# Another hand-written order for the first eleven stretches, and another way to store the last two rows, in a one-core attention kernel

## The chip, the cores and the metric

The kernel runs on one core of a Trainium2 chip. The metric is the time that the device needs for one execution, in microseconds; the profile and the trace come from one such execution, recorded by the hardware profiler. TensorE (PE) multiplies matrices, VectorE (DVE), ScalarE (ACT) and GpSimd (POOL) work on tiles, and SyncE (SP) issues most of the DMAs. ACT and POOL can issue DMAs as well.

## The reference

```python
xn = layernorm(x)                                   # x: 1 x 2048 x 640
q  = (xn @ wq).reshape(1, 2048, 32, 192)            # 32 heads of 192
k, v = k_cache[:, :, -512:], v_cache[:, :, -512:]   # a window of 512 keys
p  = softmax(q @ k.T * 192 ** -0.5)
s  = (p @ v).reshape(1, 2048, 32 * 192) @ wo
# a second branch on xn: the two tokens with the largest xn @ w_r go through a small
# gated network (640 -> 1536 -> 640) and are added back to xn
g  = silu(branch(xn))
out = x + s * g
```

All inputs are bfloat16, the sums are made in float32.

## The kernel before, in words

The 2048 tokens are 16 tiles of 128. The 32 heads are 8 groups of four, each of two pairs of heads. A step i is a group, a block of 512 tokens (four tiles) and a pair; the first steps are i = 0 and 1 for the first block and the two pairs, 2 and 3 for the second block, and so on. A step has four units, one for each token tile: unit n belongs to step n // 4. Units are taken together in stretches: S.0 has units 0 and 1, S.1 units 2 and 3, and each later stretch three units (S.2 has 4, 5, 6; S.3 has 7, 8, 9). There are 86 stretches.

Nothing is scheduled by a planner. Every engine works its instructions in the order in which the program writes them, and the program writes them by a list of short words. For the stretches 0 to 10 that list is the string `FIRST`, written by hand; from 11 on the function `stretch` writes it, and the end is again by hand (`LAST`). The words are these, with the engine in brackets; a last letter a, v or g chooses ScalarE, VectorE or GpSimd, or, for loads, the queue:

- `x.b.lo.hi`: load token tiles lo to hi of block b (SP, or ACT with an a). `k`, `v`, `wq`, `wo`: loads of the keys, the values and the two weights.
- `bn.n.c` (VectorE, half the statistics of tile n) or `as.n` (ScalarE, the statistics of tile n in two passes), `sq`, `rc`, `pw` (the inverse root), `ap.n` (the normalised tile). `sx` and `ex` load ScalarE's tables. `z` is a product of zeros on TensorE.
- `turn.n` (TensorE transposes of a tile and a copy), `xT.lo.hi` and `kT` (transposes by DMA), `kt.0` and `kt.1` (TensorE transposes of the first keys and a copy).
- `q.i.c` (a third of the projection of step i, five products with 512 columns; with lo and hi, a half with 256 columns), `qe.i.c` its eviction to `qT`.
- `S.j`: the scores of the stretch, two heads for each unit; `M.n.h` the maximum of a row (VectorE); `E.n.h` the exponential (ScalarE); `P.n` the transpose of the result by DMA (SP); `R` the reciprocal of the sums.
- `O.n` (products with the values) and `Oe.n` its eviction; `T.j` the transpose of a stretch's outputs by DMA (SP), `T.j.lo.hi` of a part of it; `W.w` (products with `wo` for a row of token tiles, two halves of 320 columns) and `We.w` the eviction into the running sum.

PSUM has eight buffers in two pools: six (`ps_p`) for scores, for both halves of a `W`, and for each `q`, `O` or `turn` that asks for one (a g on `q` and `O`), and two (`ps_f`) for the others. A buffer is given out in the written order of the words that release it: the next product that asks for one gets the buffer whose last reader stands first in the list, and waits for that reader.

The last row of token tiles is `W.127`, in three parts of 256, 192 and 192 columns; the row ahead of it is `W.126`, in two parts of 320. Their evictions are `w_out` (lines 423 to 453 of the kernel before): a product with the gate and a sum, and the store of the row to HBM.

Of the kernel before, what the change touches and what calls it, by code (L numbers as in the profile page):

```python
# [21 lines left out]
def kernel(ctx, tc, A_x, A_k_cache, A_v_cache, A_wq, A_wo, B_x, B_w_r, B_w_gate, B_w_up, B_w_down, out):  # L22
    nc = tc.nc
    P = 128
    _, S, D = A_x.shape
# [397 lines left out]
    def w_out(w, e="v"):  # L423
        b, u = divmod(w, 4)
        g, t5, _ = steps[b * PAIRS]
        n = t5 * 4 + u
        parts = w_open.pop(w)
        if g < NG - 1:
            for w_ps, lo, hi in parts:
                acc = s_acc[:, n, lo:hi]  # L430
                if g == 0:
                    copies[e](out=acc, in_=w_ps)
# [8 lines left out]
        for k, (w_ps, lo, hi) in enumerate(parts):
            cs = slice(lo, hi)
            by_v = e == "v" or last and k > 0
            prod = w_ps if by_v else t[:, cs]
            nc.vector.tensor_tensor(out=prod, in0=w_ps, in1=xn[:, n, cs], op=ALU.mult)  # L445
            if e != "g":
                (nc.vector if by_v else nc.gpsimd).tensor_tensor(out=o[:, cs], in0=prod, in1=s_acc[:, n, cs], op=ALU.add)  # L447
# [478 lines left out]
```

## The time and the profile before

| | us |
|---|---|
| median of three runs | 790.01 (789.75 to 790.72) |
| the profiled execution, time | 789.15 |
| the profiled execution, span of the trace | 787.4 |
| TensorE busy | 781.8 (99%) |
| VectorE busy | 621.7 (79%) |
| ScalarE busy | 479.4 (61%) |
| granted TensorE clock | 0.999 |

The span runs from the first to the last recorded instruction. The time of the same execution is longer by what lies around it. A busy TensorE isn't always at work: the end of a product is modelled, and a product that waits in the pipeline for a short while can be counted as busy. So in the dense part the starts of the products are read, not their busy time.

### The profile page before, as it was taken

The numbers are of one execution on the slowest core, as the hardware profiler recorded it, in microseconds if no ns is written. First come the engines' busy times: TensorE is split into PE (matmuls) and PEld (weight loads), VectorE is DVE, ScalarE is ACT, GpSimd is POOL, SyncE is SP. The second block draws the span as 40 slices with busy tenths as digits, with TensorE's granted clock in tenths as the row PEclk, the third lists the DMA queues.
The fourth block names the chain that finished last, engine by engine and source line by source line (L and its number), as shares of the span: only waits on it lengthen the run. The fifth ranks groups of instructions, "written<-read, shape, count | busy, mean of one in ns | idle before, by whom it ended". The sixth has DMA issues, their size and how long they took to land.

```text
span 787.4 us, 15694 instructions
## 1 busy us (share of the span) xinstructions
PE 781.8 (99%) x5767; PEld 482.8 (61%) x5767; DVE 621.7 (79%) x1238; ACT 479.4 (61%) x1299; POOL 179.5 (23%) x198
## 2 busy tenths in 40 slices
PE   8999999999999999999999999999999999999998
PEld 4566656666666666566666655666566666556666
DVE  7976678988888777777777777777788988777786
ACT  8975766565556655565665556565667865565652
POOL 3230000000010000000000699960000000165966
PEclk9999999999999999999999999999999999999999
DMA  9999998899889999999998899779997799997996
GB/s 262 214 202 229 204 199 132 164 175 202 166 147 219 184 195 217 142 221 198 191 222 144 181 180 188 158 141 174 202 172 138 143 193 184 183 194 152 177 167 148
DMA packets 453133, 143.80 MB, mean 183 GB/s; under 512 B 421358, under 2 KB 452720, under 8 KB 453056
## 3 DMA queue, kind: packets, MB, share of 16 engines
q1 hardware_dynamic: 447696, 138.04, 94.0%
q10 hardware_dynamic: 4672, 3.08, 1.4%
q0 software_dynamic: 688, 1.68, 0.9%
q8 instruction: 45, 0.74, 0.4%
q14 instruction: 32, 0.26, 0.1%
HBM read 39.98 MB, written 2.62 MB: 54 GB/s over the span
## 4 chain that ended last, share of the span: by engine, by line
PE 95%; DMA 2%; DVE 1%; ACT 1%; issue 0%; SPq 0%; POOL 0%; DVEq 0%
PE q_ps L317 26%; PE w_ps L420 26%; PE o_ps L372 21%; PE sc L331 14%; PE sc L338 8%; DMA oT<-o_sb 1%; DMA x_in<-in_A_x_dram 1%; ACT pexp L353 1%; DVE nm L346 0%; DVE stats L172 0%; POOL fin_o L447 0%; PE gu_ps L590 0%; ACT o_sb L385 0%; PE y_ps L627 0%; DVE fin_t L445 0%
## 5 line engine op out<-in xcount | busy, mean ns | idle before, releaser
L353 ACT ACTIVATE pexp<-sc,nm 128x512 bf16<-128x512 f32 x512 | 348.5, 697 | 264.1 <-issue 231.7
L346 DVE TENSOR_REDUCE nm<-sc 128x1 f32<-128x512 f32 x512 | 314.9, 682 | 70.9 <-PE sc L338 70.7
L317 PE MATMUL q_ps<-xnT,wq_p 128*128 128x512 bf16 (+1 forms) x985 | 225.4, 374 | 0.5 <-DMA wq_p<-in_A_wq_dram 0.5
L420 PE MATMUL w_ps<-wo_g,oT 128*128 128x320 bf16 (+1 forms) x1542 | 223.0, 298 | 0.1
L420 PEld LDWEIGHTS <-oT 128*128 128x128 bf16 x1542 | 150.4, 98 | 69.5 <-DMA oT<-o_sb 0.4
L372 PE MATMUL o_ps<-v_sb,pT 128*128 128x192 bf16 x2048 | 184.8, 246 | 0.0
L372 PEld LDWEIGHTS <-pT 128*128 128x128 bf16 x2048 | 171.4, 98 | 14.0 <-issue 2.8
L317 PEld LDWEIGHTS <-wq_p 128*128 128x128 bf16 x985 | 89.7, 98 | 122.8 <-issue 33.3
L387 DVE TENSOR_TENSOR o_sb<-o_ps,lsum 128x384 bf16<-128x384 f32 x240 | 132.0, 556 | 41.3 <-PE o_ps L372 22.7
L331 PE MATMUL sc<-kT,qT 128*128 128x512 bf16 x512 | 125.5, 379 | 0.1
L434 DVE TENSOR_TENSOR s_acc<-s_acc,w_ps 128x320 f32<-128x320 f32 x192 | 92.5, 483 | 30.7 <-PE w_ps L420 30.7
L353 ACT ACTIVATION_READ_ACCUMULATOR pexp<-sc,nm 128x1 f32 x512 | 110.2, 215 | 0.0
L309 ACT ACTIVATE qT<-q_ps 128x512 bf16<-128x512 f32 (+1 forms) x180 | 98.7, 604 | 0.0
L331 PEld LDWEIGHTS <-qT 128*128 128x128 bf16 x512 | 48.5, 98 | 42.0 <-issue 1.5
L338 PE MATMUL sc<-kT,qT 64*128 64x512 bf16 x512 | 70.2, 380 | 0.0
L338 PEld LDWEIGHTS <-qT 64*128 64x128 bf16 x512 | 18.0, 94 | 46.7 <-issue 35.8
L664 POOL TENSOR_TENSOR s_acc<-s_acc,xn 128x640 f32<-128x640 f32 x16 | 22.9, 1434 | 103.0 <-DVE s_acc L434 102.9
L643 POOL TENSOR_TENSOR xn<-xn,yh 128x640 bf16<-128x640 bf16 x32 | 44.6, 1394 | 2.7
L633 POOL DMA_DIRECT2D y_d<-y_sb x4 | 2.2, 544 | 181.2 <-DVE y_sb L630 181.2
L510 POOL DMA_DIRECT2D c_d<-cand x1 | 0.7, 725 | 162.8 <-DVE cand L508 162.8
L665 POOL TENSOR_TENSOR s_acc<-s_acc,x_fin 128x640 f32<-128x640 f32 x16 | 22.4, 1400 | 61.4 <-DVE s_acc L434 54.3
L642 POOL TENSOR_SCALAR yh<-y_bc,oh 128x640 bf16<-128x640 bf16 x32 | 25.6, 800 | 5.2 <-DMA y_bc<-y_d 3.6
(110 smaller groups left out, 234.1 us busy)
## 6 DMA issues: line engine op xcount, KB each, us to landing
wo_g<-in_A_wo_dram SPq DMA_DIRECT2D x15, 480.0 KB, 4.3
wq_p<-in_A_wq_dram SPq DMA_DIRECT2D x14, 480.0 KB, 4.6
v_sb<-in_A_v_cache_dram SPq DMA_DIRECT2D x15, 384.0 KB, 4.3
k_raw<-in_A_k_cache_dram SPq DMA_DIRECT2D x28, 192.0 KB, 3.2
pT<-pexp SPq DMA_TRANSPOSE x256, 3.6
x_fin<-in_A_x_dram SPq DMA_DIRECT2D x16, 160.0 KB, 2.7
wgu<-in_B_w_gate_dram SPq DMA_DIRECT2D x15, 128.0 KB, 3.3
wgu<-in_B_w_up_dram SPq DMA_DIRECT2D x15, 128.0 KB, 3.6
```

Source lines behind the costliest of these rows:

```text
L309: nc.scalar.activation(out=out, in_=in_, func=ACT.Copy, scale=scale)
L317: nc.tensor.matmul(q_ps, lhsT=wq_of[g * PAIRS + pr][:, dc, c * P:(c + 1) * P], rhs=xnT[:, t5 * 4 + lo:t5 * 4 + hi, dc, :], start=(dc == 0) ...
L331: nc.tensor.matmul(sc_of[n][hh], lhsT=qT_of[i][:, 2 * hh, u * P:(u + 1) * P], rhs=kp[:, :, 2 * hh, :], start=True, stop=False)
L338: nc.tensor.matmul(sc_of[n][hh], lhsT=qT_of[i][hs, 1, u * P:(u + 1) * P], rhs=kp[hs, :, 1, :], start=False, stop=True)
L346: nc.vector.tensor_reduce(out=nm_of[j][:, c:c + 1], in_=sc_of[n][hh], axis=AX.X, op=ALU.max, negate=True)
L353: nc.scalar.activation(out=pe_of[n][:, hh, :], in_=sc_of[n][hh], func=ACT.Exp, bias=nm_of[j][:, c:c + 1], scale=1.0, accum_out=l_of[j][:, ...
L372: nc.tensor.matmul(ps[:, hh, :], lhsT=pT_of[n][:, hh, jj, :], rhs=v_sb[:, hh, jj, :], start=(jj == 0), stop=(jj == NJ - 1))
L387: nc.vector.tensor_tensor(out=osb_of[j][:, m], in0=ps, in1=l_of[j][:, 2 * m:2 * m + 2].unsqueeze(2).to_broadcast([P, 2, Dh]), op=ALU.mult)
L420: nc.tensor.matmul(w_ps, lhsT=oT_of[j][:, stretches[j].index(n), c % 3, :], rhs=wo_of[g][:, c, lo:hi], start=(c == 0), stop=(c == CPG - 1))
L434: nc.vector.tensor_tensor(out=acc, in0=acc, in1=w_ps, op=ALU.add)
L642: nc.gpsimd.tensor_scalar(out=yh, in0=M["y_bc"][:, j, :], scalar1=M["oh"][:, n, j:j + 1], scalar2=0.0, op0=ALU.mult, op1=ALU.add)
L643: nc.gpsimd.tensor_tensor(out=xn[:, n, :], in0=xn[:, n, :], in1=yh, op=ALU.add)
```

## The change

`FIRST` is written in another order. The words are the same work, with few exceptions: the first block's tiles 0 and 1 come by two loads, tile 0 by ACT's queue and tile 1 by SP's; tiles 2 and 3 of the second block come in one load in place of two; `q.1.1` and `q.6.0` are split into halves and `q.1.0` no longer is; some evictions go to the other of ScalarE and VectorE, and some products to the other PSUM pool; of the loads that ACT issues late in this part, `k.3.1` and `wo.1.0` go to SP. In `w_out`, the last row's second and third parts are both multiplied ahead of their sums and are stored by one DMA, where there were two, and the row ahead of it is stored in two halves.

```diff
+        def add(k, prod, cs):
+            by_v = e == "v" or last and k > 0
+            (nc.vector if by_v else nc.gpsimd).tensor_tensor(out=o[:, cs], in0=prod, in1=s_acc[:, n, cs], op=ALU.add)
+            if last and k == 0 or w == NW - 2:
+                nc.sync.dma_start(out=out_v[:, n, cs], in_=o[:, cs])
+
+        sums = []
         for k, (w_ps, lo, hi) in enumerate(parts):
...
             if e != "g":
-                (nc.vector if by_v else nc.gpsimd).tensor_tensor(out=o[:, cs], in0=prod, in1=s_acc[:, n, cs], op=ALU.add)
-            if last:
-                (nc.scalar if k > 0 else nc.sync).dma_start(out=out_v[:, n, cs], in_=o[:, cs])
+                sums.append((k, prod, cs))
+            if not (last and k == 1):
+                for args in sums:
+                    add(*args)
+                sums = []
...
-        if not last:
+        if last:
+            nc.scalar.dma_start(out=out_v[:, n, DA:D], in_=o[:, DA:D])
+        elif w < NW - 2:
```

The part of `FIRST` ahead of S.0, and the stretches 0 to 7, which the prediction walks through:

```diff
-z.1 z.1 z.1 sx z.1 z.1 x.0.0.2 x.0.2.4 as.1 k.0.1 k.0.0 bn.0.0 bn.0.1 bn.3.0 sq.0.1 sq.1.2 as.2 rc.0.1 rc.1.2 wq.0 x.1.1.2 ap.0.v ex ap.1.v bn.3.1 pw.2.4 turn.0.v turn.1.1.v kt.0.a kt.1.v q.0.0.0.2.g qe.0.0.0.2.a ap.3.g bn.5.0 x.1.0.1 x.1.3.4 x.1.2.3 q.0.1.0.2.g k.1.1 bn.5.1 qe.0.1.0.2.a q.0.2.0.2.g k.1.0 qe.0.2.0.2.a turn.3.1.a as.6 ap.2.v bn.7.0 bn.7.1 turn.2.v 
-S.0 bn.4.0 v.0 bn.4.1 wq.1 q.0.0.2.4.g qe.0.0.2.4.a x.2.0.4 kT.1 M.0.0 E.0.0 pw.4.8 q.0.2.2.4.g M.0.1 qe.0.2.2.4.v E.0.1 P.0 q.0.1.2.4 qe.0.1.2.4.a M.1.0 M.1.1 E.1.0 E.1.1 ap.4.v 
-S.1 q.1.2 ap.5.g M.2.0 ap.7.g E.2.0 M.2.1 q.1.0.2.4 ap.6.g xT.4.6 q.1.0.0.2.g bn.10.0 qe.1.2.a M.3.0 M.3.1 R.0 bn.10.1 xT.6.8 E.2.1 qe.1.0.0.2.a qe.1.0.2.4.a q.1.1 P.2 bn.11.0 O.0 bn.11.1 bn.8.0 E.3.0 E.3.1 qe.1.1.a Oe.0.v P.1 bn.8.1 
-S.2 x.3.0.4 v.1 q.2.1.0.2 as.9 M.4.0 M.4.1 q.2.0 M.6.0 E.4.0 pw.8.12 E.4.1 q.2.2.g M.5.0 qe.2.1.0.2.a E.5.0 qe.2.0.v M.6.1 ap.10.g E.6.0 ap.9.g P.3 E.6.1 M.5.1 q.3.1 qe.2.2.v ap.8.v R.1 ap.11.g O.2 qe.3.1.v Oe.2.v E.5.1 
-S.3 M.8.0 M.7.0 P.4 P.5 M.8.1 q.2.1.2.4 M.7.1 R.2 xT.8.10 M.9.0 as.13 bn.15.0 M.9.1 E.8.0 E.7.0 E.8.1 q.3.2 bn.14.0 xT.10.12 E.7.1 P.6 qe.2.1.2.4.a q.3.0.g qe.3.0.a qe.3.2.v E.9.0 E.9.1 O.1.g O.5.g O.4.g Oe.4.a Oe.1.v P.8 as.12 Oe.5.v O.3 
-S.4 P.7 bn.15.1 M.10.0 q.4.1 M.11.0 M.12.0 M.11.1 Oe.3.a q.4.0 P.9 M.10.1 qe.4.1.v E.10.0 M.12.1 E.11.0 T.0 E.11.1 q.5.0.g E.10.1 wo.0.0 wo.0.1 T.2.0.1 E.12.0 E.12.1 R.3 qe.4.0.a O.8.g O.7 P.10 Oe.7.a qe.5.0.v T.1 Oe.8.v R.4 bn.14.1 pw.12.16 
-S.5 ap.12.g O.6 M.13.0 P.11 E.13.0 M.15.1 Oe.6.a M.15.0 E.15.0 E.15.1 q.4.2 M.13.1 P.12 q.5.2.g M.14.1 M.14.0 qe.4.2.v O.9 E.13.1 Oe.9.a qe.5.2.v E.14.0 W.0 We.0.v E.14.1 
-S.6 M.17.0 P.13 M.17.1 ap.14.g M.16.1 O.10 M.18.1 Oe.10.a M.16.0 ap.13.g E.17.0 q.5.1 E.17.1 qe.5.1.v T.2.1.3 E.16.0 R.5 O.12 O.11.g Oe.11.a M.18.0 E.18.0 Oe.12.a E.16.1 W.1 O.13.g We.1.v E.18.1 ap.15.g xT.13.16 xT.12.13 W.2 We.2.v P.15 Oe.13.a 
+z.1 x.0.0.1.a sx bn.0.0 x.0.1.2 as.1 x.0.2.4 bn.0.1 x.1.0.1 sq.0.1 bn.3.0 z.1 k.0.0 rc.0.1 sq.1.2 z.1 rc.1.2 z.1 ap.0.v ap.1.v k.0.1 bn.3.1 bn.4.0 z.1 as.2 turn.1.1.a turn.0.v ex pw.2.4 kt.0.v wq.0 kt.1.a x.1.1.2 x.1.2.4 ap.3.v q.0.0.0.2.g q.0.2.0.2.g q.0.1.0.2.g qe.0.0.0.2.a k.1.0 bn.4.1 bn.7.0 bn.7.1 ap.2.g k.1.1 qe.0.2.0.2.a bn.5.0 qe.0.1.0.2.a turn.2.1.a wq.1 turn.3.1.v 
+S.0 bn.5.1 q.0.2.2.4.g M.0.0 as.6 pw.4.8 E.0.0 M.0.1 q.0.0.2.4.g E.0.1 qe.0.2.2.4.v v.0 q.0.1.2.4 qe.0.1.2.4.a ap.4.g qe.0.0.2.4.v M.1.0 E.1.0 ap.6.g x.2.0.4 q.1.1.0.2 M.1.1 E.1.1 
+S.1 qe.1.1.0.2.a ap.5.v M.2.0 M.3.0 E.2.0 kT.1 M.2.1 bn.8.0 q.1.0.g ap.7.g qe.1.0.a q.1.1.2.4.g P.0 bn.10.0 M.3.1 E.3.0 E.2.1 R.0 bn.11.0 q.1.2 xT.4.6 xT.6.8 P.2 qe.1.1.2.4.v qe.1.2.a E.3.1 bn.10.1 O.0 Oe.0.a bn.11.1 
+S.2 M.4.0 M.4.1 bn.8.1 q.2.1.0.2 q.2.0 as.9 P.1 E.4.0 M.5.0 x.3.0.4 M.5.1 v.1 pw.8.12 q.2.2.g E.4.1 qe.2.0.v ap.10.g E.5.0 P.4 E.5.1 P.3 M.6.0 qe.2.2.a E.6.0 qe.2.1.0.2.v q.3.1.g M.6.1 O.2 q.2.1.2.4.g P.5 E.6.1 qe.2.1.2.4.a ap.8.g qe.3.1.v ap.11.g R.1 Oe.2.v ap.9.v 
+S.3 M.7.0 q.3.2 M.7.1 M.9.0 xT.8.10 as.13 E.7.0 M.8.0 M.9.1 O.4 q.3.0.g E.7.1 xT.10.12 qe.3.2.a R.2 O.3.g E.8.0 M.8.1 O.1.g E.9.0 O.5 Oe.4.v qe.3.0.a E.9.1 P.6 E.8.1 Oe.3.v P.7 P.8 Oe.1.v bn.15.0 Oe.5.v 
+S.4 bn.15.1 T.0 q.4.1 M.10.0 as.14 M.12.1 M.12.0 E.10.0 R.3 q.4.0 M.11.0 E.12.0 P.9 qe.4.0.v E.12.1 qe.4.1.a q.5.0.g O.7 E.11.0 wo.0.0 M.10.1 wo.0.1 bn.12.0 E.10.1 T.2.0.1 M.11.1 qe.5.0.v E.11.1 O.8 
+S.5 bn.12.1 Oe.7.a pw.12.16 P.10 Oe.8.a M.13.0 M.15.0 T.1 P.12 M.13.1 O.6 q.4.2 E.13.0 Oe.6.v P.11 q.5.2.g M.14.0 M.15.1 E.13.1 O.9 E.14.0 M.14.1 R.4 E.14.1 W.0 qe.5.2.a qe.4.2.v ap.15.g O.10 E.15.0 We.0.v ap.12.g Oe.9.v E.15.1 Oe.10.v 
+S.6 T.2.1.3 M.16.0 O.12 ap.14.g M.17.0 q.5.1 ap.13.a E.16.0 Oe.12.v M.16.1 P.13 P.15 xT.12.13 M.17.1 M.18.1 M.18.0 E.16.1 E.17.0 O.11 E.17.1 W.1 E.18.0 E.18.1 R.5 W.2 We.1.a xT.13.16 Oe.11.v We.2.v P.14 qe.5.1.v T.3 
+S.7 M.19.0 M.20.0 O.13 Oe.13.a E.19.0 T.4 q.6.1 k.2.1.a M.21.0 q.6.2 qe.6.1.v P.16 qe.6.2.a O.14.g M.21.1 M.19.1 E.21.0 M.20.1 q.7.0 E.19.1 Oe.14.v E.20.0 E.21.1 qe.7.0.a O.15 P.17 E.20.1 q.6.0.0.2.g W.4 W.3 P.18 Oe.15.v q.6.0.2.4 qe.6.0.0.2.a P.19 We.4.a We.3.a 
...
```

More of the change, by code (lines that the diff above doesn't have):

```diff
@@ L440, in w_out @@
         o = fin_pool["o"].tile([P, D], BF16, name="fin_o")
+        def add(k, prod, cs):
[4 more added lines that the diff above has]
+        sums = []
         for k, (w_ps, lo, hi) in enumerate(parts):
             cs = slice(lo, hi)
-            by_v = e == "v" or last and k > 0
-            prod = w_ps if by_v else t[:, cs]
+            prod = w_ps if e == "v" or last and k > 0 else t[:, cs]
             nc.vector.tensor_tensor(out=prod, in0=w_ps, in1=xn[:, n, cs], op=ALU.mult)
             if e != "g":
-                (nc.vector if by_v else nc.gpsimd).tensor_tensor(out=o[:, cs], in0=prod, in1=s_acc[:, n, cs], op=ALU.add)
-            if last:
-                (nc.scalar if k > 0 else nc.sync).dma_start(out=out_v[:, n, cs], in_=o[:, cs])
+                sums.append((k, prod, cs))
[3 more added lines that the diff above has]
+                sums = []
         if e == "g":
             nc.gpsimd.tensor_tensor(out=o, in0=t, in1=s_acc[:, n, :], op=ALU.add)
-        if not last:
+        if last:
+            nc.scalar.dma_start(out=out_v[:, n, DA:D], in_=o[:, DA:D])
+        elif w < NW - 2:
             (nc.gpsimd if w < NW - 8 else nc.scalar if w < NW - 6 else nc.sync).dma_start(out=out_v[:, n, :], in_=o)
@@ L876 @@
-S.7 q.6.1 M.19.1 M.19.0 E.19.0 M.20.0 q.6.0 qe.6.0.v P.14 T.4 M.21.0 M.20.1 M.21.1 E.19.1 T.3 q.6.2.g k.2.1.a qe.6.1.a O.14 O.15.g R.6 E.20.0 q.7.1.g E.20.1 Oe.14.a P.17 qe.6.2.a E.21.0 Oe.15.v q.7.0 P.16 E.21.1 P.19 W.3 P.18 W.4 qe.7.1.v R.7 qe.7.0.v We.3.v O.19 We.4.a wq.2.a
-S.8 wq.3.a O.16 Oe.19.v M.22.0 v.2.a M.23.1 E.22.0 Oe.16.v k.3.0.a M.23.0 P.20 E.23.0 wo.1.0.a E.23.1 k.3.1.a T.5 M.22.1 M.24.0 P.21 q.7.2 E.24.0 O.17 Oe.17.v E.22.1 P.22 k.2.0.a W.5 qe.7.2.v M.24.1 We.5.a O.20 P.23 W.6 O.21 We.6.a E.24.1 Oe.20.a Oe.21.a O.18.g Oe.18.v P.24
@@ new lines @@
+S.6 T.2.1.3 M.16.0 O.12 ap.14.g M.17.0 q.5.1 ap.13.a E.16.0 Oe.12.v M.16.1 P.13 P.15 xT.12.13 M.17.1 M.18.1 M.18.0 E.16.1 E.17.0 O.11 E.17.1 W.1 E.18.0 E.18.1 R.5 W.2 We.1.a xT.13.16 Oe.11.v We.2.v P.14 qe.5.1.v T.3
+S.7 M.19.0 M.20.0 O.13 Oe.13.a E.19.0 T.4 q.6.1 k.2.1.a M.21.0 q.6.2 qe.6.1.v P.16 qe.6.2.a O.14.g M.21.1 M.19.1 E.21.0 M.20.1 q.7.0 E.19.1 Oe.14.v E.20.0 E.21.1 qe.7.0.a O.15 P.17 E.20.1 q.6.0.0.2.g W.4 W.3 P.18 Oe.15.v q.6.0.2.4 qe.6.0.0.2.a P.19 We.4.a We.3.a
+S.8 qe.6.0.2.4.a O.19 M.22.0 T.5 k.2.0.a M.23.0 wq.2.a q.7.1 M.22.1 k.3.0.a R.6 M.23.1 E.22.0 v.2.a E.22.1 M.24.0 P.21 qe.7.1.v P.20 q.7.2.g E.23.0 E.23.1 E.24.0 M.24.1 W.5 We.5.v qe.7.2.v O.16.g E.24.1 k.3.1 wq.3.a Oe.16.v W.6 R.7 O.18.g O.17.g Oe.18.v Oe.19.a Oe.17.v O.21 We.6.a
@@ L880 @@
+S.9 Oe.21.v wo.1.0 M.25.1 O.20 M.27.1 M.25.0 q.8.1 P.22 Oe.20.a E.25.0 P.23 M.26.0 P.24 M.27.0 T.6 q.8.0 E.25.1 M.26.1 qe.8.1.v P.25 T.7 W.7 E.27.0 E.27.1 We.7.v P.27 E.26.0 E.26.1 q.9.0
+S.10 P.26 qe.9.0.a qe.8.0.v M.28.0 O.22 kT.2 R.8 M.28.1 O.23 E.28.0 q.8.2.g Oe.22.v M.30.0 qe.8.2.v E.28.1 O.24.g Oe.23.a M.29.0 Oe.24.v P.28 E.29.0 M.30.1 R.9 T.8 kT.3 E.30.0 O.25 M.29.1 E.30.1 Oe.25.v E.29.1 W.9 P.30 W.8 O.26.g P.29 O.27.g v.3 We.8.a Oe.26.v wo.1.1 Oe.27.v We.9.a T.9.2.3 T.9.0.2
     """.split()
```

2 lines of the change are left out of this document (removed).

## The prediction

> **What bounds the kernel now.** I read the page first: its engine rows and its chain of waits.
>
> ```profile
> PE 781.8 (99%) x5767; PEld 482.8 (61%) x5767; DVE 621.7 (79%) x1238; ACT 479.4 (61%) x1299; POOL 179.5 (23%) x198
> PE 95%; DMA 2%; DVE 1%; ACT 1%; issue 0%; SPq 0%; POOL 0%; DVEq 0%
> ```
>
> The chain is TensorE for 95% of the span. The change gives TensorE the same products, so it can only move the time at which the first projection starts, the waits between products up to stretch 11, and the end behind the last product. Next I took the timeline of TensorE around the first projection and at S.11, and the chain in a calm place behind it.
>
> ```profile
> 8.61 1.81 PE L317 MATMUL q_ps<-xnT,wq_p 128*128 128x256 bf16 x15 [0.45 <-DMA wq_p<-in_A_wq_dram]
> ...
> 10.88 1.03 PE L331 MATMUL sc<-kT,qT 128*128 128x512 bf16 x4
> ...
> 12.38 1.81 PE L317 MATMUL q_ps<-xnT,wq_p 128*128 128x256 bf16 x15
> 14.02 1.36 PE L331 MATMUL sc<-kT,qT 128*128 128x512 bf16 x4
> 15.31 0.61 PE L338 MATMUL sc<-kT,qT 64*128 64x512 bf16 x4
> ...
> 98.45 1.46 PE L331 MATMUL sc<-kT,qT 128*128 128x512 bf16 x6
> ```
>
> ```profile
> 104.56 1.98 PE o_ps L372 x24
> 106.54 1.29 PE sc L331 x6
> ...
> 108.59 2.26 PE q_ps L317 x10
> 110.85 1.63 PE w_ps L420 x12
> ```
>
> From the second fence, with no wait in it: an O takes 1.98 / 3 = 0.66 us, a W 1.63. A stretch of three units and two projections take 110.85 - 106.54 = 4.31; one undisturbed projection is 1.08 (half of 2.26 less the 0.1 that a group loses when it follows scores), so the stretch itself is 2.15. S.0 and S.1 are 12.38 - 10.88 = 1.50 each. Between the first projection and S.11 the list has, before and after alike, projections worth 28 whole ones, 28 O, 10 W, S.0 to S.10 and two turns (0.57 together, 10.88 - 10.31): 30.2 + 18.5 + 16.3 + 3.0 + 19.4 + 0.6 = 88.0. The trace takes 98.45 - 8.61 = 89.8. **All waits of this part are worth 1.8 us.** That is the most an order can bring here, unless the first projection starts sooner; 0.2% of 790 is 1.6 us, about what a measurement of this kernel can tell from no change.
>
> **The start.** The first projection waited for its weights, 0.45 us in the row at 8.61. They are the fifth load on SP's queue, and the queue's bytes set when they land.
>
> ```profile
> 2.74 0.43 SPq L112 DMA_DIRECT2D wq_p<-in_A_wq_dram  x1
> 4.50:8.60 4.10, 3.40 (x34) 1.89 (x32) 3.60 (x12) 4.02 (x11) 1.19 (x4) 1.00 1.04 344
> DMA to landing us min/median/max: 5.8/5.8/5.8
> ```
>
> Issued at 2.74, landed 5.8 later, with the 16 DMA engines all busy (1.04) at 344 GB/s. Ahead of `wq.0` stood 320 + 320 + 192 + 192 KB; in the new order it is 160 + 160 + 320 + 160 + 192 + 192 KB, one tile of 128 x 640 x 2 bytes = 164 kB more, or 164 / 344 = 0.48 us. If the two queues start the stream sooner by the 0.45 that one issue takes, little of it remains: bounds 0 and +0.48. I take **+0.35**, nearer to the upper end since the engines are saturated in the row. The Trainium skill's page "DMA: Bandwidth & Descriptors", section "Issuing engines are not separate DMA queues", says that queues of SP, ACT and GpSimd share the same 16 engines and that spreading loads over them saves only issue time; by that rule the term is +0.48 and the sum below 0.13 higher. No run here has loads on two queues in this phase, so the trace can't settle it.
>
> **S.0 and S.1.** I walk the new order by hand: a step starts when its engine is through with the step ahead and its inputs are there.
>
> ```profile
> 12.83 1.24 DVE L346 TENSOR_REDUCE nm<-sc 128x1 f32<-128x512 f32 x2
> 13.98 0.41 DVE L307 TENSOR_SCALAR qT<-q_ps 128x256 bf16<-128x256 f32 x1
> ...
> 15.51 0.77 DVE L260 TENSOR_SCALAR xn<-x_in,mv,rstd 128x640 bf16<-128x640 bf16 x1
> ```
>
> VectorE has as many statistics ahead of `M.0.0` as before, and it, not TensorE, sets 12.83. In the old order S.1's first four products took 1.36 for S.0's 1.03: they waited for the eviction at 13.98 and ScalarE's behind it. The new order puts `q.1.1.0.2` (0.54) between, so S.1 is due at 14.02 + 0.35 + 0.54 = 14.9, when the evictions are through (two maxima to 14.0, two half evictions to 14.7). **-0.33.**
>
> **S.1 to S.2.**
>
> ```profile
> 15.92 2.28 PE q_ps L317 x15
> ...
> 18.23 1.24 PE q_ps L317 x5
> 19.47 0.80 PE o_ps L372 x8
> ```
>
> Four projections and an O are 3.24 + 0.66 = 3.90; here 2.28 + 0.04 + 1.24 + 0.80 = 4.36, 0.1 of it the step out of the scores: two waits, 0.34 together, for buffers and for `P.0`. In the new order they stand later against E.1.0 and E.1.1, which free the buffers. **-0.34.** But then the second product of S.2 needs `qe.1.2`, which is now behind three exponentials and `qe.1.0` on ScalarE.
>
> ```profile
> 20.59 0.64 ACT L309 ACTIVATE qT<-q_ps 128x512 bf16<-128x512 f32 x1
> 21.07 0.78 ACT L242 ACTIVATE junk_a<-x_in 128x640 bf16<-128x640 bf16 x1
> ...
> 22.81 0.69 ACT L353 ACTIVATE pexp<-sc,nm 128x512 bf16<-128x512 f32 x1
> ...
> 23.49 0.68 ACT L353 ACTIVATE pexp<-sc,nm 128x512 bf16<-128x512 f32 x1
> ```
>
> VectorE: 14.7, two maxima to 15.9, `ap.5` 0.77 to 16.6, `M.2.0` to 17.2. ScalarE from 17.25: three exponentials of 0.67 and two evictions of 0.6 end at 20.45. TensorE is there at 16.4 + 2.7 + 0.66 + 0.22 = 19.98. **+0.47.** Behind it ScalarE has E.3.1, `Oe.0` (now its own, two copies, about 0.75) and `as.9` (21.07 to 22.81, 1.7): E.4.0 begins at 23.5, not at 22.81. `q.2.2` takes the buffer that E.4.0 frees and is due at 24.0, freed at 24.25: **+0.25.**
>
> **S.3 to S.6.** In the old order this is where the chain left TensorE.
>
> ```profile
> 34.26 1.80 PE L331 MATMUL sc<-kT,qT 128*128 128x512 bf16 x6
> ...
> 36.82 1.47 PE L317 MATMUL q_ps<-xnT,wq_p 128*128 128x512 bf16 x6
> ...
> 41.38 1.68 PE L331 MATMUL sc<-kT,qT 128*128 128x512 bf16 x6
> ...
> 43.75 0.42 PE L372 MATMUL o_ps<-v_sb,pT 128*128 128x192 bf16 x3
> ...
> 54.08 2.02 PE L420 MATMUL w_ps<-wo_g,oT 128*128 128x320 bf16 x12
> 55.94 0.49 PE L372 MATMUL o_ps<-v_sb,pT 128*128 128x192 bf16 x4
> ```
>
> ```profile
> 39.09 2.87 DMA oT<-o_sb
> ...
> 42.08 0.57 DVE o_sb L387
> ...
> 50.08 4.59 DMA oT<-o_sb
> ```
>
> S.4 took 36.82 - 34.26 = 2.56 for 2.15: 0.41 of waits for buffers and `xT.10.12`. In the new order I find 0.05 at S.3 and 0.15 at S.4 (E.8.1 frees its fourth buffer at 35.4): **-0.21.** `T.0` was issued at 39.09 behind `P.9`; its landing held `Oe.8`, and S.5 waited for the buffer: 43.75 - 41.38 = 2.37 for 2.15. It now stands ahead of `P.9` and lands by 41, while `Oe.7` is due at 42.4: **-0.22.** `T.2.1.3` was issued at 50.08 behind `P.13` and held W.1: 55.94 - 54.08 = 1.86 for 1.63; it now stands ahead, at about 47.3: **-0.23.**
>
> **S.7 to S.10.** S.7's third to sixth score products get the buffers of W.1 and W.2, by the order of release. `We.1` is now ScalarE's, behind six exponentials.
>
> ```profile
> 69.75 0.43 ACT L432 COPY s_acc<-w_ps 128x320 f32<-128x320 f32 x1 [1.85 <-PE w_ps L420]
> 80.98 1.02 PE sc L331 x4
> ```
>
> E.18.1 ends at 57.0, the two copies of 0.43 and their drain at 58.1; the fourth product is due at 57.9 less the earlier gains. **+0.40.** At S.9 the old row has 1.02 for four products of 0.216 (1.29 / 6): a wait of 0.16 for `Oe.18`, whose O now comes earlier: **-0.16.** S.8 and S.10 come out without a wait.
>
> **The end.**
>
> ```profile
> 784.53 0.36 DVE L447 TENSOR_TENSOR fin_o<-w_ps,s_acc 128x192 bf16<-128x192 f32 x1
> ...
> DMA to landing us min/median/max: 1.5/1.6/1.8
> ```
>
> The second part's sum filled the time in which VectorE waited for the third part's product; moved behind, the last sum still starts at about 784.5. One store of 384 columns leaves when the second store of 192 left. Those of 192 columns took 1.5 to 1.6, those of 640 took 1.8: **+0.1.** The half stores of the row ahead are off the path: the last store of a whole row, issued at 783.9, landed well ahead of the end.
>
> **Sum.** 0.35 - 0.33 - 0.34 + 0.47 + 0.25 - 0.21 - 0.22 - 0.23 + 0.40 - 0.16 + 0.1 = +0.1. I add 0.1 for waits a walk by hand doesn't see: +0.2. The profiled execution took 789.15, 1.75 over its span, and would take 789.35; the median lies 0.86 above it, so I say **790.2**. Unknown lengths (the start 0.5, each of the five places at S.2, S.4 and S.7 by 0.3) give this case its own range of 788.9 to 791.5.
>
> **Rivals.** *SP's queue turns late (slower).*
>
> ```profile
> 23.82 6.06 SPq L358 DMA_TRANSPOSE pT<-pexp  x3
> 29.98 2.97 SPq L271 DMA_TRANSPOSE xnT<-xn  x2
> ```
>
> Three P took 6.06 where others take 1.4 each: one issue was stretched by 1.8 while `x.3` and `v.1` moved. In the new order the first of them is `P.4`, which waits for E.4.1 until 24.9 (0.7 on ScalarE behind E.4.0's 24.2); P.3, P.5 and both xT are 1.0 later. `q.4.1` began at 36.82, as the second xT landed. If two P are stretched, it lands at 36.8 + 1.0 + 1.8 = 39.6, and TensorE, due at 37.0, loses 2.6; `T.0` and `T.2.1.3` are late as well and give back 0.45: 790.2 + 3.0 = **793.2**. It decides from a landing at 37.9 on. For it: SP has no slack there. Against: the loads are as early as before. 22%.
>
> *ScalarE as the owner of PSUM (slower).* `We.1`, `We.3` and `We.8` are now ScalarE's, and S.7, S.8 and S.11 wait for them. If ScalarE is 0.7 later than I walked at each, it is 2.1: **792.3**. For it: at S.7 it already holds. Against: ScalarE is busy only 61%. 10%.
>
> *All waits go (faster).* The two queues hide the extra tile, and the places at S.2 and S.7 don't wait: -1.8 and +0.1, **788.3**. Against: the order of ScalarE at S.2 is plain in the list. 10%. That the change does nothing at all is my forecast in effect: 58%.
>
> **How the numbers follow.** Faster by over 0.2%: 10%; within: 58%; slower: 22 + 10 = 32%. The range runs from the forecast's lower end, 788.7 with some of the fast case, to 792.8 with most of both slow ones.
>
> **What would show it.** The first projection at 8.9 to 9.1; S.1 with no gap between its first four products; a gap of about 0.5 behind S.2's first; `q.4.1` at 37; S.7's fourth product late; S.11 at 98.4 to 98.7; the last store landing 1.6 us after its issue. I am wrong if S.11 starts beyond 100 or ahead of 97.

## The result, and the profile after

The changed kernel takes 792.28 us (median of 22 executions, 789.81 to 794.84), the kernel before 790.08 (22 executions, 789.26 to 791.31); the ratio is 1.0030, interval 1.0022 to 1.0038. The forecast was 790.2 with a range to 792.8: the time lies in the range, but on the side of "slower by over 0.2%", which had 32%, not in the 58%. The profiled execution took 792.55, its span is 790.7, 3.4 over the 787.4 of before. The medians are only 2.2 apart; the profiled execution of before, 789.15, lies 0.9 under its median. From the page of the changed kernel, the engines' busy time, the engines' shares of the chain of waits, and three groups (the last field is the idle time ahead of the group and what ended it):

```profile
PE 781.0 (99%) x5772; PEld 483.5 (61%) x5772; DVE 622.8 (79%) x1241; ACT 478.1 (60%) x1289; POOL 178.8 (23%) x197
PE 92%; DMA 4%; DVE 1%; ACT 1%; SPq 1%; ACTq 0%; issue 0%; DVEq 0%
L420 PE MATMUL w_ps<-wo_g,oT 128*128 128x320 bf16 (+1 forms) x1542 | 222.7, 298 | 0.4 <-ACT pexp L353 0.4
L372 PE MATMUL o_ps<-v_sb,pT 128*128 128x192 bf16 x2048 | 185.1, 246 | 1.3 <-DMA pT<-pexp 1.3
L331 PE MATMUL sc<-kT,qT 128*128 128x512 bf16 x512 | 124.8, 379 | 1.7 <-ACT s_acc L432 1.7
```

The same three groups of before:

```profile
L420 PE MATMUL w_ps<-wo_g,oT 128*128 128x320 bf16 (+1 forms) x1542 | 223.0, 298 | 0.1
L372 PE MATMUL o_ps<-v_sb,pT 128*128 128x192 bf16 x2048 | 184.8, 246 | 0.0
L331 PE MATMUL sc<-kT,qT 128*128 128x512 bf16 x512 | 125.5, 379 | 0.1
```

TensorE has the same work; 3% of the chain moved from it, mostly to DMA. The three groups now have idle time ahead of them, and each of these is a single place in the trace. TensorE's timeline of the changed kernel:

```profile
9.46 1.81 PE L317 MATMUL q_ps<-xnT,wq_p 128*128 128x256 bf16 x15 [1.03 <-DMA wq_p<-in_A_wq_dram]
...
15.36 1.03 PE L331 MATMUL sc<-kT,qT 128*128 128x512 bf16 x4
...
16.85 2.88 PE L317 MATMUL q_ps<-xnT,wq_p 128*128 128x512 bf16 x15
21.00 0.83 PE L372 MATMUL o_ps<-v_sb,pT 128*128 128x192 bf16 x8 [1.28 <-DMA pT<-pexp]
...
35.77 1.46 PE L331 MATMUL sc<-kT,qT 128*128 128x512 bf16 x6
...
38.10 3.41 PE L317 MATMUL q_ps<-xnT,wq_p 128*128 128x512 bf16 x15
...
42.67 1.46 PE L331 MATMUL sc<-kT,qT 128*128 128x512 bf16 x6
...
44.82 0.83 PE L372 MATMUL o_ps<-v_sb,pT 128*128 128x192 bf16 x8
...
75.66 1.79 PE L420 MATMUL w_ps<-wo_g,oT 128*128 128x320 bf16 x12 [0.37 <-ACT pexp L353]
...
81.56 0.59 PE L331 MATMUL sc<-kT,qT 128*128 128x512 bf16 x2
83.90 1.14 PE L331 MATMUL sc<-kT,qT 128*128 128x512 bf16 x4 [1.75 <-ACT s_acc L432]
```

O.0 waits at 21.00 for P.0, W.5 at 75.66 and the scores of S.9 at 83.90 for ScalarE. To sum the waits I take the undisturbed lengths of the prediction for all words (O 0.66, W 1.63, a stretch 2.15 or 1.50, a projection 1.08) from the time between two marks; what is left is waits:

| us | first projection starts | waits from there to S.7 | waits from S.7 to O.27 (the last O of S.10) | O.27 to the end |
|---|---|---|---|---|
| before | 8.61 | 1.74 | 0.17 | 689.59 |
| after | 9.46 | 1.73 | 2.59 | 689.70 |

The differences 0.85, 0.0, 2.4 and 0.1 are the 3.4 of the span. Up to S.7 gains and losses cancel; S.8 and S.9 are where the change loses. The traces of the experiments below agree. Up to S.7 six traces with the changed order (after, e1, e7, e9, e10, e11) have 1.7 to 3.0 of waits and three with the old one (before, e2, e8) 1.7 to 2.9. From S.7 to O.27 four with the changed words of that part (after, e4, e7, e11) have 1.1 to 2.6, and four with the old ones (before, e2, e3, e8) 0.17 each.

The words of S.8 in the changed kernel:

```
S.8 qe.6.0.2.4.a O.19 M.22.0 T.5 k.2.0.a M.23.0 wq.2.a q.7.1 M.22.1 k.3.0.a R.6 M.23.1 E.22.0 v.2.a E.22.1 M.24.0 P.21 qe.7.1.v P.20 q.7.2.g E.23.0 E.23.1 E.24.0 M.24.1 W.5 We.5.v qe.7.2.v O.16.g E.24.1 k.3.1 wq.3.a Oe.16.v W.6 R.7 O.18.g O.17.g Oe.18.v Oe.19.a Oe.17.v O.21 We.6.a
```

The chain of waits of the changed kernel for that place (start, length, what):

```profile
73.23 9.07 DMA pT<-pexp
82.30 0.02 issue
82.32 0.38 ACTq L112
...
82.80 0.73 ACT o_sb L385 x2
83.53 0.32 ACT s_acc L432
...
83.90 1.14 PE sc L331 x4
```

The transpose P.20, issued at 73.23, takes 9.07 to land. The load `wq.3` on ScalarE's queue (L112) is issued 0.02 after that landing: it reuses P.20's completion semaphore (the trace shows eight, shared by all DMAs of SP and ScalarE). In ScalarE's order `Oe.19` and `We.6` stand behind this load, and We.6 owns the PSUM buffer that the third score product of S.9 is given. ScalarE did no work from 78.3 until then.

### The profile page after: what moved, and what is told of

Same layout as the page of the kernel before. It is cut to its first block, busy times and chain, and to the rows that moved or that the text cites. A ratio compares the mean times of both kernels' runs of the same rounds, so it can differ in the third digit from the quotient of the medians.

```text
span 790.7 us, 15698 instructions
## 1 busy us (share of the span) xinstructions
PE 781.0 (99%) x5772; PEld 483.5 (61%) x5772; DVE 622.8 (79%) x1241; ACT 478.1 (60%) x1289; POOL 178.8 (23%) x197
## 3 DMA queue, kind: packets, MB, share of 16 engines
q10 hardware_dynamic: 3744, 2.56, 1.3%
## 4 chain that ended last, share of the span: by engine, by line
PE 92%; DMA 4%; DVE 1%; ACT 1%; SPq 1%; ACTq 0%; issue 0%; DVEq 0%
PE w_ps L420 26%; PE q_ps L317 25%; PE o_ps L372 20%; PE sc L331 13%; PE sc L338 8%; DMA pT<-pexp 2%; DMA x_in<-in_A_x_dram 1%; DMA xnT<-xn 1%; DVE nm L346 1%; ACT pexp L353 0%; DVE stats L172 0%; PE gu_ps L600 0%; SPq L101 0%; ACTq L124 0%; SPq L271 0%
## 5 line engine op out<-in xcount | busy, mean ns | idle before, releaser
L387 DVE TENSOR_TENSOR o_sb<-o_ps,lsum 128x384 bf16<-128x384 f32 x249 | 137.0, 556 | 39.3 <-PE o_ps L372 20.2
L309 ACT ACTIVATE qT<-q_ps 128x512 bf16<-128x512 f32 (+1 forms) x182 | 100.7, 606 | 1.1 <-PE q_ps L317 1.1
```

Of the source, the lines that this page charges most:

```text
L309: nc.scalar.activation(out=out, in_=in_, func=ACT.Copy, scale=scale)
L387: nc.vector.tensor_tensor(out=osb_of[j][:, m], in0=ps, in1=l_of[j][:, 2 * m:2 * m + 2].unsqueeze(2).to_broadcast([P, 2, Dh]), op=ALU.mult)
```

## The experiments

Each result is the median, then its ratio to the kernel before with the 95% interval. A trace is of one execution, so a wait that goes from the trace need not lower the median by as much.

**S.9: one load moved (e1).** The changed kernel with

```diff
-S.8 ... k.3.1 wq.3.a Oe.16.v ... O.21 We.6.a
+S.8 ... k.3.1 Oe.16.v ... O.21 We.6.a wq.3.a
```

> The changed kernel with one word moved: the load wq.3.a is issued by ScalarE behind We.6.a and no longer ahead of Oe.19.a and We.6.a. Queue theory (ScalarE stood at 77.5 to 82.3 because this load waits for a DMA semaphore that P.20's landing at 82.30 frees, and S.9's last buffers wait for We.6.a behind it): the wait of 1.9 us inside S.9 goes, at most a small one at q.9.0 for the later weights takes its place, and the median falls by 1.4 to 1.9, from 792.3 to 790.4 to 790.9. Rival (S.9 waits for PSUM buffers because ScalarE has too much work, or for the transposes P.20 to P.22, whatever stands in its queue): S.9 keeps 1 us or more of its wait and the median stays within 0.6 of 792.3.

792.14 us, 1.0018 (1.0008 to 1.0029): the median fell by 0.1, not by the 1.4 to 1.9 expected. In the trace the wait in S.9 is gone: the stretch takes its undisturbed time, though P.20 again landed only at 82.05. `wq.3`, now behind We.6, was issued at 82.30, 0.02 after the landing of `k.3.1`, whose semaphore it reuses here. So it was ScalarE, held by the load, that stopped S.9. But W.5 now waited 1.3, and 1.9 of the 2.6 from S.7 to O.27 stayed. TensorE's and ScalarE's timelines:

```profile
77.03 1.79 PE L420 MATMUL w_ps<-wo_g,oT 128*128 128x320 bf16 x12 [1.13 <-ACT pexp L353]
...
82.92 1.46 PE L331 MATMUL sc<-kT,qT 128*128 128x512 bf16 x6
```

```profile
75.77 0.38 ACTq L133 DMA_DIRECT2D v_sb<-in_A_v_cache_dram  x1
76.20 0.69 ACT L353 ACTIVATE pexp<-sc,nm 128x512 bf16<-128x512 f32 x1 [1.59 <-DMA oT<-o_sb]
```

Here the load `v.2` holds ScalarE in the same way, for the landing of the turn T.5, and E.22.1 behind it frees the buffer that W.5 needs.

**The end alone (e2).** The list `FIRST` of before with the new `w_out`.

> The old order of the first eleven stretches with the new stores of the last two rows. Prediction: the last store of 384 columns lands 0.1 us later after the same issue time, so +0.1 (790.1 to 790.3). Rival (the half stores or the moved products matter): more than 0.3 us either way.

790.06 us, 1.0002 (0.9993 to 1.0011): the end is neutral.

**The two halves of the list (e3, e4).** e3 has the new order ahead of S.0 and in S.0 to S.2, the old one behind; e4 the reverse (both with the old `w_out`).

> The new order up to and including stretch 2, the old one from stretch 3 on (without P.4, P.5 and the half projection that are already done), the old stores. Head theory (0.85 us of later weights and the wait of 1.4 us before O.0 are the head's own): 1.0 to 1.8 us over the kernel before, 791.1 to 791.9, and no wait at S.9. Rival (the head's lateness is absorbed behind it, and all of the loss is from stretch 7 on): within 0.4 of the kernel before.

> The old order up to and including stretch 2, the new one from stretch 3 on (with P.4, P.5 and a half projection that the new one has earlier), the old stores. If the queue theory holds and the two parts add, S.9 waits for 1.9 and W.5 for 0.5 here, less what the new order saves at S.4, S.5 and W.1 (0.6): 1.2 to 2.0 over the kernel before, 791.3 to 792.1. Rival (the loss is the head's): 0.3 to 0.8 us faster than the kernel before.

e3: 793.2 us, 1.0039 (1.0026 to 1.0052), over the 791.1 to 791.9 expected; e4: 791.14, 1.0012 (1.0003 to 1.0020), just under the 791.3 to 792.1 expected. By the medians the new head alone costs as much as the whole change and the rest 0.9, so the two halves don't add up. e3's trace has the wait for P.0 (1.4), 0.17 from S.7 to O.27, and 1.2 more than before between S.11 and S.15, where no word differs; TensorE's largest idle time there is

```profile
125.62 0.84 PE L331 MATMUL sc<-kT,qT 128*128 128x512 bf16 x2 [0.55 <-DVE o_sb L387]
```

e4's has 0.1 for P.0, 1.10 from S.7 to O.27, 0.4 more than before between S.11 and S.15, and 1.9 at O.4, which is partly the hybrid's own. Before and after take the same time between S.11 and S.15; why others take longer isn't known. e3's profiled execution, 790.84, was its shortest, so what made its median isn't seen, and with it what the head costs. The first projection began at 8.32 with the new head and at 9.13 with the old one: the 0.85 of the table isn't the order's.

**P.0 and the queue "instruction" (e7, e8).** In both kernels a single packet of 16 KB, on a queue that the page calls "instruction", begins between 14 and 18 us. Around its end DMA nearly stops. The rate in 40 slices of 14 to 21 us (0.175 us each), with the median time from issue to landing of kT.1: of before,

```profile
GB/s 373 408 272 250 284 243 116 85 63 29 28 29 193 293 288 290 294 268 293 285 291 293 266 272 252 233 219 214 197 192 155 135 221 222 212 206 212 209 187 199
kT<-k_raw SPq DMA_TRANSPOSE x1, 5.7
```

of after,

```profile
GB/s 363 350 322 360 310 328 184 162 148 101 70 41 37 186 276 73 0 0 4 7 10 10 9 136 293 285 276 287 297 284 293 329 261 274 205 16 9 7 107 295
q14 instruction: 1, 0.01, 0.3%
kT<-k_raw SPq DMA_TRANSPOSE x1, 6.9
```

and of e8:

```profile
GB/s 336 366 402 351 357 370 332 301 250 158 94 25 29 15 19 249 291 294 285 297 342 279 211 53 1 0 7 9 9 10 9 234 288 274 288 291 290 290 293 285
kT<-k_raw SPq DMA_TRANSPOSE x1, 7.8
```

Behind the last large load of that phase, `x.2.0.4`, come the transposes kT.1 and P.0. In 13 traces with that order of the queue, kT.1 lands 1.24 to 1.42 after the load where the packet is through before the load has landed (before, e2, e4), and 2.71 to 2.85 after it in the ten others (after, e1, e3, e7 to e12, e14). Two kernels were to move the packet. e7 is the changed kernel with twelve tiny products of zeros more; e8 the kernel before with five zero products less:

```diff
-z.1 x.0.0.1.a sx ...
+z.1 y.12 x.0.0.1.a sx ...          # e7: y.12 = twelve products with 16 columns
-z.1 z.1 z.1 sx z.1 z.1 x.0.0.2 ... 
+sx x.0.0.2 ...                     # e8
```

> The changed kernel with twelve tiny products of zeros (16 columns each) more behind the first one, while TensorE has nothing else to do. Nothing else moves; only the queue "instruction" brings its first 16 KB some 24 TensorE instructions earlier in the program, at about 13.4 us in place of 15.0. Theory (the packet stops the DMA transposes while it lasts, and the new order puts it on kT.1 and P.0): it now falls into the bulk loads, kT.1 lands within 1.5 of x.2.0.4, O.0 waits 0.1 in place of 1.4; S.2 may show up to 0.5 for its projection's eviction, so the time is 791.0 to 791.4 (the changed kernel 792.3). Rival (the new order itself makes the transposes late: its loads and the wait for the exponential): O.0 still waits 1.3 or more and the time stays at 792.3.

> The kernel before without its five words z.1 (zero products, 512 columns, on an idle TensorE). Ten TensorE instructions less: the first 16 KB of the queue "instruction" come at about 15.3 in place of 14.3, when the loads are nearly through and kT.1 is next. Theory (packet against transposes): kT.1 and P.0 land about 1 us later (18.6 and 19.5), O.0 waits 1.0 in place of 0.1, and the time is 790.9 to 791.2 (before 790.1). Rival: the packet costs nothing, O.0 waits 0.1, 790.1. A third thing that could show: without the zero products the granted clock is lower at the first turns, and the first projection is later; then the start of the first projection says so.

e8: 790.55 us, 1.0007 (0.9998 to 1.0016). The packet began at 17.5, kT.1 landed at 19.6 and P.0 at 20.5, 2 us later than before where 1 was expected; yet O.0 waited 0.6 rather than 1.0, because TensorE was itself 0.6 late: without the zero products the first turns of the keys took 107 ns each instead of 56, and the trace's first record of a granted clock of 1.00 is at 10.0, in before at 4.7. The time moved too little to be told from none. e7: 792.41 us, 1.0037 (1.0023 to 1.0051), a miss: the packet began at 16.8, not 13.4, P.0 landed at 20.95 and O.0 waited 2.4. So the packet doesn't come at a fixed count of instructions, and I can't place it; e14 below has it at 15.6 with the head of before. What the traces show is the cost: some 1.4 us on transposes that are under way, and P.0 is on TensorE's path in the new order, where O.0 is due 10.1 after the first projection, 0.6 sooner than before.

The rate of the changed kernel has a second stop, 16 9 7 7 from 20.1 to 20.8. Ahead of it stands a packet of 8 KB on another "instruction" queue, the row q14, which the views of before and e8 don't have. In the eight traces with the new head and `x.2.0.4` in its place (after, e1, e3, e7, e9 to e12) this packet begins at 18.5 to 19.6, and P.0 lands 1.5 to 1.7 behind kT.1. In the five with the old head (before, e2, e4, e8, e14) it begins at 27.1 or later, and P.0 lands 0.8 to 1.1 behind kT.1. So some 0.7 of P.0's lateness comes with the new head every time, whenever the 16 KB come; that the small packet causes it isn't shown.

**Another load in v.2's place, alone and with the tiny products (e9, e10).**

```diff
-S.8 ... E.22.0 v.2.a E.22.1 ... k.3.1 wq.3.a Oe.16.v ...
+S.8 ... E.22.0 E.22.1 wq.3.a ... k.3.1 Oe.16.v ...
-S.9 ... M.27.0 T.6 q.8.0 ...
+S.9 ... M.27.0 T.6 v.2 q.8.0 ...
```

> The changed kernel; in S.8 the load wq.3 on ScalarE stands behind E.22.1, in the place that v.2 had one word earlier, and v.2 goes to SP in S.9 behind T.6. So no load on ScalarE waits for the landing of P.20 at 82.3, and none stands ahead of E.22.1. Theory (a load that waits for its DMA semaphore holds ScalarE, and with it PSUM): the wait in S.9 (1.9 + 0.1) and that at W.5 (0.5) both go, S.9 to S.10 takes 9.0 to 9.7; the time is 790.0 to 790.8. Rival (the bulk loads make P.20 to P.22 late whatever the load order, and another step waits for those): S.8 to S.10 keep 1.5 or more of waits somewhere else, and the time is 791.8 to 792.3.

> Both edits: the twelve tiny products at the start and wq.3 in v.2's place. Theory: the two places are all that the new order loses; with both gone its gains at S.1, S.4, S.5 and W.1 are left, 789.0 to 789.6, faster than before by 0.06 to 0.14%. Rival: a wait that goes in one place comes back in the next, 790.1 to 791.

e9: 793.0 us, 1.0025 (1.0012 to 1.0039); e10: 791.7, 1.0021 (1.0012 to 1.0029). In e9 the wait in S.9 went, 0.8 stayed at W.5, and S.7 to O.27 had 0.84 of waits in place of 2.59. The time didn't follow, and 790.0 to 790.8 was expected: a new wait stands in its profiled execution behind O.27, and the granted clock (the third number from the end) is halved behind it. TensorE's timeline and two windows of e9:

```profile
108.97 2.74 PE L372 MATMUL o_ps<-v_sb,pT 128*128 128x192 bf16 x16 [2.16 <-DMA pT<-pexp]
```

```profile
109.00:110.00 1.00, 1.00 (x7) 0.95 (x8) 0.00 (x0) 0.00 (x0) 0.00 (x0) 0.50 1.03 344
110.00:112.00 2.00, 2.00 (x13) 1.63 (x12) 0.81 (x2) 0.00 (x0) 0.00 (x0) 0.50 1.44 201
```

P.29 was issued at 104.31 and took 4.6, with the loads `v.3` and `wo.1.1` issued at 105.7 and 106.3. In e10, which reached S.8 at the same time as the changed kernel, O.19 waited 0.9 for P.19 and W.5 1.5 for T.5 and a buffer: the rival's case, the wait that comes back in the next place, though its time is over the rival's 791 too.

**v.3 and wo.1.1 later (e11).** The changed kernel with `v.3 wo.1.1` behind `T.9.0.2` in S.10.

> The changed kernel with the loads v.3 and wo.1.1 at the end of S.10 moved behind T.9.2.3 and T.9.0.2 on SP's queue. In the profile of the experiment before, O.29 waited 2.16 us for P.29, which was issued at 104.31, took 4.6 to land among these two loads, and the granted clock was 0.61 for the 4 us behind it; in the changed kernel's own profile P.29 is issued at 103.29 and lands 3.2 later, just in time. Theory (this wait comes in some of the executions, and makes their spread of 789.8 to 794.8): P.29 always lands within 3.5 of its issue; the executions lie within 790 to 792.6, the median at 791.2 (1 us under the changed kernel). Rival (the spread has another cause, such as the start or S.8): 792.3, spread as before.

792.34 us, 1.0028 (1.0016 to 1.0040), six executions from 791.36 to 793.56, where a median of 791.2 was expected. P.29 landed in 3.3, but the median didn't move; that the wait for P.29 makes the changed kernel's spread isn't shown. Its waits from S.7 to O.27 are 2.53, as in the changed kernel.

**The loads of S.8 by GpSimd (e12).** e11 with `k.2.0`, `wq.2`, `k.3.0`, `v.2` and `wq.3` as `.g`.

> The kernel of the run above (v.3 and wo.1.1 late), and the five loads that ScalarE issues in S.8 (k.2.0, wq.2, k.3.0, v.2, wq.3) are issued by GpSimd, which has nothing else to do there. So ScalarE waits for no landing of an earlier DMA. Theory (ScalarE held by its loads' waits): S.8 to S.10 without the waits at W.5 (0.5 to 1.3) and in S.9 (2.0); S.7 to the last O of S.10 takes 40.0 to 40.4 in place of 42.6; 789.6 to 790.2. Rival (the traffic of the loads itself makes P.19 to P.22 and the turns late): that stretch stays above 41.5 and the time is within 0.5 of the run above. GpSimd's own queue may also be slower at issuing: then kT.2 or q.8 would wait in S.10.

800.3 us, 1.0135 (1.0116 to 1.0154). S.7 to O.27 has only 0.22 of waits, as the theory said, but the test doesn't separate it from its rival: GpSimd was free, and issued four of the loads at 48 to 51 us. There they met other transposes; TensorE's timeline of e12:

```profile
62.70 5.78 PE L420 MATMUL w_ps<-wo_g,oT 128*128 128x320 bf16 x21 [5.91 <-DMA oT<-o_sb]
```

T.2.1.3 was issued at 49.79 and landed at 62.65, and the granted clock was 0.50 from 58.4 to 68.7. The loads took the cost with them.

**Two turns moved in the kernel before (e14).** The best-supported gains of the new order alone:

```diff
-S.4 ... q.4.0 P.9 M.10.1 qe.4.1.v E.10.0 M.12.1 E.11.0 T.0 E.11.1 ...
+S.4 ... q.4.0 T.0 P.9 M.10.1 qe.4.1.v E.10.0 M.12.1 E.11.0 E.11.1 ...
-S.6 M.17.0 P.13 ... qe.5.1.v T.2.1.3 E.16.0 ...
+S.6 M.17.0 T.2.1.3 P.13 ... qe.5.1.v E.16.0 ...
```

> The kernel before with two words moved: T.0 ahead of P.9 in S.4, and T.2.1.3 ahead of P.13 in S.6, as the new order has them. Theory: the waits of 0.22 in S.5 and 0.23 at W.1 go (S.4 to S.7 takes 23.5 in place of 24.0), 789.6 to 789.8, 0.05% below the kernel before, at the edge of what can be measured; the place in the trace decides. Rival: P.9 or P.13, now 1.4 later on SP, holds O.9 or O.13 instead, 790.1 to 790.4.

791.96 us, 1.0031 (1.0016 to 1.0046): slower, where 789.6 to 789.8 was expected. Both waits went (S.5 from 0.23 to 0.0, S.6 from 0.23 to 0.01), and 2.8 came up in S.8, where no word had been moved. TensorE's timeline of e14, its DMA issues of 69 to 75 us, and the rate in 40 slices of that time, of before and of e14:

```profile
77.30 1.40 PE L420 MATMUL w_ps<-wo_g,oT 128*128 128x320 bf16 x9 [0.98 <-DMA oT<-o_sb]
...
82.42 1.49 PE L372 MATMUL o_ps<-v_sb,pT 128*128 128x192 bf16 x16 [1.44 <-DMA pT<-pexp]
```

```profile
pT<-pexp SPq DMA_TRANSPOSE x2, 7.6
oT<-o_sb SPq DMA_TRANSPOSE x1, 7.8
```

```profile
GB/s 195 224 215 208 152 103 172 210 244 239 75 31 0 0 0 9 9 10 10 9 155 292 288 285 368 353 323 333 333 333 328 333 328 304 278 288 317 335 352 364
GB/s 164 128 144 222 224 205 203 317 205 142 65 26 0 0 0 7 9 10 9 10 82 280 287 282 218 278 287 195 118 154 53 53 191 145 179 97 307 328 323 328
```

Seven loads, of which the first is issued at 70.73, stand in S.8. T.5, issued 1.25 ahead of it, took 7.8; in the kernel before it was issued 1.92 ahead of the loads and took 4.6. P.21 took 10.4, before 7.0. No load on ScalarE's queue holds an engine in this chain: TensorE waits for the transposes themselves. But the lead ahead of the loads doesn't decide alone: in the changed kernel T.5 was issued 0.89 ahead of the first load and took 4.9.

What fits all the traces is another packet of 16 KB. In both rates above DMA nearly stops from 70.7 to 72.0, behind such a packet at 70.33 (before) and 70.17 (e14). SP was through with the issue of T.5 at 70.16 in before, but only at 71.84 in e14. In the ten traces where T.5's issue was over when this stop began, T.5 took 4.5 to 5.9; in the three where it wasn't (e7, e10, e14) 6.4 to 7.8. (e12 has other loads there.) No run moves the packet alone, so how the cost divides between it and the loads stays open; by the first reading or the second, the old order stood close to an edge. Why SP was 0.8 later at P.20 while TensorE was 0.2 later at S.7 I didn't find.

**The loads spread out (e15).** The changed kernel with three edits: `x.2.0.4` behind `P.0` (`bn.8.0 bn.10.0` behind `R.0`); of the seven loads only wq.2, wq.3 and k.2.0 left in S.8, the others behind T.6, T.7, P.26 and kT.3; `v.3 wo.1.1` behind `T.9.0.2`.

> The changed kernel with three edits at three places. (1) x.2.0.4 behind P.0 on SP's queue (and bn.8.0, bn.10.0 behind R.0), so that kT.1 and P.0 stand ahead of the last large load. (2) The seven loads of S.7 to S.9 spread out: in S.8 only wq.2, wq.3 (both ScalarE, wq.3 behind E.22.1) and k.2.0 (SP) are left; k.3.0 goes behind T.6, k.3.1 behind T.7, v.2 behind P.26, wo.1.0 behind kT.3, all on SP. (3) v.3 and wo.1.1 behind T.9.0.2. Theory (transposes that are in flight together with large loads land late, and TensorE waits for them): P.0 lands at 18.5 or earlier and O.0 waits 0.3 or less; P.20 and P.21 land within 5 us of their issue, and S.7 to the last O of S.10 takes 40.1 to 40.8; from the first projection to that O the waits are 1.3 to 2.0 in all, as many as in the kernel before, or fewer; 789.0 to 790.3. Rival for (1): x.2.0.4 now holds xT.4.6 and the projections of S.2, which wait 0.5 to 1 in place of O.0. Rival for (2): P.20, P.21 and the turns are late whatever else is loaded, since their own chain is late; S.7 to O.27 stays at 41.5 or more, 791.5 to 792.5.

796.32 us, 1.0074 (1.0060 to 1.0088). TensorE's timeline of e15, the DMA issues of 69 to 75 us of the changed kernel and of e15, and a window of e15:

```profile
18.90 0.82 PE L372 MATMUL o_ps<-v_sb,pT 128*128 128x192 bf16 x8
19.56 1.21 PE L331 MATMUL sc<-kT,qT 128*128 128x512 bf16 x4
23.14 0.59 PE L331 MATMUL sc<-kT,qT 128*128 128x512 bf16 x2 [2.37 <-DVE qT L307]
...
83.05 1.46 PE L331 MATMUL sc<-kT,qT 128*128 128x512 bf16 x6
...
90.73 1.46 PE L331 MATMUL sc<-kT,qT 128*128 128x512 bf16 x6
```

```profile
pT<-pexp SPq DMA_TRANSPOSE x3, 8.8
pT<-pexp SPq DMA_TRANSPOSE x3, 5.7
```

```profile
25.00:27.00 2.00, 2.00 (x8) 0.99 (x7) 1.97 (x5) 1.65 (x5) 0.63 (x2) 0.50 0.92 159
```

In its place (2) holds for the waits: with three loads in place of seven the transposes take 5.7 in place of 8.8 (5 or less was expected), with a stop behind a packet of 16 KB in both traces (72.0 to 73.4, and 73.7 to 75.1), S.9 takes its plain 7.68 (90.73 - 83.05), and the waits from S.7 to O.27 are 0.03. (1) holds in its first half: P.0 lands at 18.08 and O.0 doesn't wait. But the rival of (1) holds too, by another way: `x.2.0.4` lands at 21.5, VectorE's statistics wait for it, and S.2's fifth score product waits 2.4 for an eviction on VectorE; behind that the clock is halved for some 3 us, so S.2 costs 4.4. In (3) O.29 waited 3.3 for P.29, which I had put behind the load wo.1.0. The span is 7.4 over that of before: 0.2 of it is the start, 2.7 are waits up to S.7 and 4.6 lie behind O.27, while S.7 to O.27 has 0.1 less. No version here beats the kernel before.

## Why the forecast came out on the wrong side, step by step

The time lies in the range because the range took in two slow rivals. The one that came had its mechanism right but not its places, and the other cost 0.2 and not its 2.6, so the time inside the range says little for the walk.

**What bounds it: right.** All waits of before up to S.11 were put at 1.8; the same sum to O.27 is 1.9. TensorE's work is the same, and time moved only through its waits.

**The start, +0.35: not there.** The 0.85 of the profiled execution is chance. `wq.0` landed at 8.53 on the mean of five traces with the old head, at 8.60 on that of nine with the new one. By the rule that I took from the Trainium skill's page "DMA: Bandwidth & Descriptors" (section "Issuing engines are not separate DMA queues") I had worked out an estimate of +0.48; the 0.07 that the traces show doesn't bear that out here.

**S.0 and S.1, -0.33: right.** S.1 takes 1.49 (16.85 - 15.36), without a gap.

**S.1 to S.2, -0.34: the first step that failed.** I let both waits of that place go because E.1.0 and E.1.1 stand later; of P.0 I looked at when it is issued and needed, not at when it lands. It was issued at 15.44, 0.46 later than before, and landed 5.5 after its issue instead of 3.6, behind kT.1 and with both packets; O.0 waited 1.4. The same wait covered the next two terms: the +0.47 for `qe.1.2` didn't show (where O.0 did not wait, in e15, it was 0.17), and neither did the +0.25 behind E.4.0.

**S.3 to S.6, -0.66: right.** S.4 takes 2.33 (38.10 - 35.77) where it took 2.56, S.5 2.15 (44.82 - 42.67) where it took 2.37, and the W of S.6 are without a wait; e14 shows the last two as the work of the two moved turns.

**S.7 to S.10: the step that cost the forecast.** S.7's +0.40 for We.1 isn't there. "S.8 and S.10 come out without a wait" and "-0.16" at S.9 became +0.5 at W.5 and +1.9 in S.9 (2.02 with the place behind). I walked the engines' work in these stretches but gave the loads on ScalarE's queue no length at all: neither what they wait for before they are issued, nor what their 1.8 MB do to the transposes beside them. Three experiments take waits away in this place by moving loads alone: e1 the wait in S.9, e12 and e15 both. That the loads hold ScalarE is shown by e1 and by the semaphores. How much of the transposes' length is the loads' and how much the packet's stays open, and in none of the three did the median come down to the kernel before.

**The end, +0.1: right.** The one store of 384 columns took 1.64 from issue to landing, the last one of before 1.53, and e2 is neutral.

**The rivals.** "SP's queue turns late" was decided from `xT.10.12` landing at 37.9; it landed at 38.06 and `q.4.1` lost 0.2, not 2.6. "ScalarE as the owner of PSUM" had the mechanism and a price of 2.1, but We.1, We.3 and We.8 as its places and ScalarE's own work as its reason; it was We.6 and E.22.1, on an idle ScalarE, behind a load. Its 10% was too low, since the profile of before already showed seven loads on ScalarE's queue in S.8 with 4 to 6 us to land. The two together had 32%. The mark that I set for being wrong, S.11 beyond 100, was met: it starts at 101.71.

## What to carry to other kernels

A load in the program of an engine that also evicts is a wait of that engine, for the landing of whatever DMA used its semaphore last: when words move, list for each such load what it waits for, and who stands behind it. A transpose by DMA has no fixed length: here a P takes 3.3 us alone, and transposes take 5 to 13 us beside large loads and packets of the queue "instruction". Spreading the loads out brought it from 8.8 to 5.7 in e15; that an earlier issue would do as well isn't shown. And a gain of 0.2 in one place moves every later one against transfers that keep their own time, as in e14, so it's the next tight place that says what the gain is worth.
